# Attention scores with the mask added by a matmul and two heads in one product over 128 rows

## The chip, the core and the metric

The kernel runs on one core of a Trainium2 chip. The metric is the device time of one execution in microseconds (us). TensorE (PE) multiplies matrices and writes its results to PSUM; VectorE (DVE), ScalarE (ACT) and GpSimd (POOL) work elementwise; SyncE (SP) issues the DMAs. Each engine takes its instructions in the order of its own queue and waits on semaphores for the others.

## What is computed

Three stages follow each other: an attention over windows, a mixture of experts and a dense feed-forward layer. The change is in the first.

```python
# q, k, v: (4, 8, 576, 64), float32
scores = np.matmul(q, k.transpose(0, 1, 3, 2)) / np.sqrt(64)
rel = pos[:, None] - pos[None, :]
mask_plain = (rel >= 0) & (rel < 32)                     # heads 0 to 3
mask_dil = (rel >= 0) & (rel < 128) & (rel % 4 == 0)     # heads 4 to 7
scores = np.where(masks, scores, -1e9)
attn = np.exp(scores - scores.max(-1, keepdims=True))
attn = attn / (attn.sum(-1, keepdims=True) + 1e-9)
x = np.matmul(attn, v)          # then 2304 tokens x 512
# x: eight experts with gates normalised 8 times over rows and columns; then relu(x @ w_in)**2 @ w_out
```

## The kernel before

The host sorts positions by their remainder modulo 4 for the heads with the dilated mask, so that both masks become a band over neighbours. The 576 queries of a head are cut into 18 blocks of 32, and a block sees 64 keys (its own 32 and the 32 ahead). A *group* is one batch, four heads and six blocks; there are 4 x 2 x 3 = 24 groups.

`slot(i)` is the loop of the attention stage. It records, for different groups, the scores of group i (`att_scores`, L393), the exponential and the normalisation of group i - 1 (`att_exp`, `att_norm`), the product with v of group i - 3 (`att_pv`, L442), the transposes of group i - 2 (`att_tr`, L432), and matmuls that fill: either warm-ups on zeros (L999) or the first products of the experts (L587). Then SP gets the loads: q and k two groups ahead (`load_qk`), v (`load_v`), and parts of the expert weights or of the mask. The order in which the code is written is the order of each queue; no planner moves anything.

In `att_scores` each head of each block is a matmul of its own. Its rows are the 64 dimensions of the head, so heads 0 and 2 use rows 0 to 63 of the array and heads 1 and 3 rows 64 to 127, each with 32 columns. That is 24 products per group, and in float32 each is two matmuls with a weight load each; the trace counts 48. The weights are the 32 queries, the data that stream through are 64 keys, and the result is a PSUM tile `s` of 128 rows (4 heads x 32 queries) by 6 x 64, of which two banks rotate. On DVE, L413 scales the scores and adds the mask, a tile of 128 rows in SBUF with 0 or -1e30, and writes `ms`; L417 takes the maximum of each row. POOL subtracts it (L418) and ACT takes the exponential (L422). DVE sums (L427), adds 1e-9 (L428) and inverts (L429); POOL multiplies (L430). PE transposes (L437), ACT copies to `pts`, PE multiplies by v into `xt` (L452), and ACT copies the result into `xf` (L484), for the dilated heads at a step of 4 floats.

The mask comes in four pieces, the first ahead of the loop and three in slots 0 to 2. After the loop come the gates and then some 1800 us of expert and feed-forward products, nearly all of them PE's.

Of the kernel before, what the change touches and what calls it, by code (L numbers as in the profile page):

```python
# [10 lines left out]
F32 = mybir.dt.float32  # L11
F32R = mybir.dt.float32r
I32 = mybir.dt.int32
U32 = mybir.dt.uint32
AF = mybir.ActivationFunctionType
ALU = mybir.AluOpType
AX = mybir.AxisListType
PSUM = bass.MemoryType.PSUM

B, H, S, D = 4, 8, 576, 64  # L20
NTOK, DM = B * S, H * D
E, FE, FF = 8, 1024, 2048
QB = 32
PAD = 32
KB = QB + PAD
NB = S // QB
GB = 6
NM = NB // GB
QC = GB * QB
# [14 lines left out]
NEG = -1e30  # L44
# [4 lines left out]
def tile_kernel(ctx: ExitStack, tc: tile.TileContext, a):  # L49
    nc = tc.nc  # L50
    out = a["out"]
# [8 lines left out]
    xfp = att.enter_context(tc.tile_pool(name="xfp", bufs=1))  # L60
    qkv = att.enter_context(tc.tile_pool(name="qkv", bufs=2))
# [19 lines left out]
    every = slice(0, KC)  # L81

    ident = const.tile([128, 128], F32, name="ident")
    mask = xfp.tile([128, 4 * GB, KB], F32, name="mask")
    wg = xfp.tile([128, KC, 32], F32, name="wg")
    warm = xfp.tile([128, 128], F32, name="warm")

# [9 lines left out]
    bufs = {"s": 2, "xt": 2, "pt": 1, "mm": 3}  # L97
# [279 lines left out]
    q_t, k_t, v_t, e_t, pt_t, xt_t = {}, {}, {}, {}, {}, {}  # L377

    def load_qk(i):
        if i < NG:  # L380
            b, hg, m = groups[i]
            q_t[i] = qkv.tile([128, 2, QC], F32, tag="q", name="q", bufs=3)
            nc.sync.dma_start(q_t[i], a["q"][b, hg, m])
            k_t[i] = qkv.tile([128, 2, KCOLS], F32, tag="k", name="k", bufs=3)
            nc.sync.dma_start(k_t[i], a["k"][b, hg, m])

    def load_v(i):
        if i < NG:
            b, hg, m = groups[i]
            v_t[i] = qkv.tile([128, GB // 2, 4 * D], F32, tag="v", name="v", bufs=4)  # L390
            nc.sync.dma_start(v_t[i], a["v"][b, hg, m])

    def att_scores(i):  # L393
        _, hg, m = groups[i]
        qt, kt = q_t.pop(i), k_t.pop(i)
        ps = psum.tile([128, 512], F32, tag="s", name="s")[:, :GB * KB].rearrange("p (g k) -> p g k", g=GB)
        for g in range(GB):
            for head in range(4):
                pr, rows = head // 2, slice(D * (head % 2), D * (head % 2) + D)
                nc.tensor.matmul(  # L400
                    ps[QB * head:QB * head + QB, 2 * (g % 3) + g // 3, :],
                    qt[rows, pr, g * QB:g * QB + QB],
                    kt[rows, pr, g * QB:g * QB + KB],
                    start=True,
                    stop=True,
                )
        ms = at.tile([128, GB, KB], F32, tag="ms", name="ms", bufs=5)
        if hg == 0 and m > 0:
            mk = mask[:, 2:3, :].to_broadcast([128, GB, KB])
        else:  # L410
            k = m + 1 if hg else 0
            mk = mask[:, GB * k:GB * k + GB, :]
        nc.vector.scalar_tensor_tensor(  # L413
            out=ms, in0=ps, scalar=1.0 / float(np.sqrt(D)), in1=mk, op0=ALU.mult, op1=ALU.add,
        )
        mx = at.tile([128, GB, 1], F32, tag="mx", name="mx", bufs=3)
        nc.vector.tensor_reduce(out=mx[:, :, 0], in_=ms, axis=AX.X, op=ALU.max)  # L417
        nc.gpsimd.tensor_tensor(out=ms, in0=ms, in1=mx.to_broadcast([128, GB, KB]), op=ALU.subtract)  # L418
        e_t[i] = ms

    def att_exp(i):
        nc.scalar.activation(out=e_t[i], in_=e_t[i], func=AF.Exp)  # L422

    def att_norm(i):
        ex = e_t[i]
# [54 lines left out]
    def att_x(i):  # L480
        _, hg, _ = groups[i]
        for half, xt in enumerate(xt_t.pop(i)):
            for c, w, t0, step in att_parts(i, half):
                nc.scalar.copy(xf(slice(2 * hg, 2 * hg + 2), t0, w, step), xt[:, :, c:c + w])  # L484
# [444 lines left out]

    with tc.manual_schedule():  # L930
        nc.vector.memset(warm, 0.0)
        load_qk(0)
        nc.sync.dma_start(mask[:, :GB], a["mask"][:, :GB])
        load_qk(1)
        load_qk(2)
        nc.sync.dma_start(ident, a["ident"])

        ps = psum.tile([128, 512], F32, tag="s", name="s")
# [57 lines left out]
        def warm_up(n):  # L996
            ps = bank("mm") if n else None
            for _ in range(n):
                nc.tensor.matmul(ps, wr, xr, start=True, stop=True)  # L999
# [9 lines left out]
        def preparing(i):  # L1009
            for i0, z in ops:  # L1010
                if i >= i0:
                    next(z, None)
            for f in prep0.get(i, ()):
                f()

        def slot(i):
            if i < NG:
                att_scores(i)
            if 0 <= i - 4 < NG:
                att_x(i - 4)  # L1020
            if 0 <= i - 1 < NG:
                att_exp(i - 1)
                att_norm(i - 1)
            if 0 <= i - 3 < NG:
                att_pv(i - 3)
            between.get(i, lambda: None)()
            preparing(i)
            if 0 <= i - 2 < NG:
                att_tr(i - 2)
            for _ in range(filled.get(i, 0)):  # L1030
                next(filling)
            warm_up((4 if i < 6 else 2 if i < per + 4 else 3 if i < NG else 6) - filled.get(i, 0))
            if i:
                load_qk(i + 2)
            load_v(i)
            if parts:
                parts.pop(0)()
            if i < 3:
                cols = slice(GB * i + GB, GB * i + 2 * GB)
                nc.sync.dma_start(mask[:, cols], a["mask"][:, cols])  # L1040
            if i == 3:
                nc.sync.dma_start(wg, a["w_gate"])
            if i == 2:
                load_parts(0, 0)
            if i == 6:
                load_parts(0, 1)
            if i == 15:
                load_parts(1, 0)
# [194 lines left out]
def _layout(x):  # L1243
    q, k, v = x["q"], x["k"], x["v"]

    def order(z):
        lo = z[:, :4]
        hi = z[:, 4:].reshape(B, 4, S // DIL, DIL, D).transpose(0, 1, 3, 2, 4).reshape(B, 4, S, D)
        return np.stack([lo, hi], axis=1)

    qo, ko, vo = order(q), order(k), order(v)

    def pairs(z):
        return z.reshape(B, 2, 2, 2, S, D).transpose(0, 1, 3, 5, 2, 4)

    qs = pairs(qo).reshape(B, 2, 128, 2, NM, QC).transpose(0, 1, 4, 2, 3, 5)
    kz = pairs(ko).reshape(B, 2, 128, 2, S)
    kz = np.concatenate([np.zeros((B, 2, 128, 2, PAD), kz.dtype), kz], axis=-1)
    ks = np.stack([kz[..., m * QC:m * QC + KCOLS] for m in range(NM)], axis=2)

    vp = np.concatenate([np.zeros((B, 2, 4, PAD, D), v.dtype), vo], axis=3)
    vt = np.stack([vp[:, :, :, j * QB:j * QB + KB] for j in range(NB)], axis=3)
    vt = vt.reshape(B, 2, 4, NM, 2, GB // 2, KB, D).transpose(0, 1, 3, 4, 6, 5, 2, 7)
    vt = vt.reshape(B, 2, NM, 128, GB // 2, 4 * D)

    def first(w, n):
        return w.reshape(KC, 128, n, FC, 128).transpose(2, 1, 3, 0, 4).reshape(n, 128, KC * FB)

    def second(w, n):
        return w.reshape(n, FC, 128, DM).transpose(0, 2, 1, 3).reshape(n, 128, FC * DM)  # L1270

    w1 = np.concatenate([first(x["moe_w1"][e], SPE) for e in range(E)])
    w2 = np.concatenate([second(x["moe_w2"][e], SPE) for e in range(E)])
    kk = np.arange(KB)[None, :]
    qq = np.arange(QB)[:, None]
    band = (kk > qq) & (kk <= qq + PAD)

    def split_at(o):
        return band & ((qq < o) | (kk >= PAD + o))

    first_block, split, after_split = split_at(0), split_at(QB // 2), band & (kk >= QB // 2)
    masks = [
        z[3 * (k % 2) + k // 2]
        for z in (
            [first_block] + [band] * 5,
            [first_block, band, band, band, split, after_split],
            [band, band, band, first_block, band, band],
            [band, split, after_split, band, band, band],
        )
        for k in range(GB)  # L1290
    ]
    arrays = {
        "q": qs,
        "k": ks,
        "v": vt,
        "w_gate": np.pad(x["moe_w_gate"].reshape(KC, 128, E).transpose(1, 0, 2), ((0, 0), (0, 0), (0, 32 - E))),
        "w1": w1,
        "w2": w2,
        "w_in": first(x["moe2_w_in"], NS2),
        "w_out": second(x["moe2_w_out"], NS2),  # L1300
        "mask": np.tile(np.stack([np.where(m, 0.0, NEG).astype(np.float32) for m in masks], axis=1), (4, 1, 1)),
        "ident": np.eye(128, dtype=np.float32),
    }
    arrays = {n: np.ascontiguousarray(z) for n, z in arrays.items()}
    for n in ("w_in", "w_out"):
        arrays[n] = arrays[n].view(np.int64)
    return arrays
# [16 lines left out]
```

## Time and profile before

| | us |
|---|---|
| median of 3 runs (lowest, highest) | 1931.33 (1928.61, 1933.84) |
| the profiled execution | 1931.37 |
| its span | 1929.6 |
| PE busy in the span | 1902.9 (99%) |
| DVE busy | 1626.1 (84%) |
| ACT busy | 745.9 (39%) |
| POOL busy | 634.6 (33%) |

The profile was taken in one execution. A row that begins with a line number or an engine stands for instructions; `x` counts them. In a group of instructions the two numbers behind the bar are the busy time and the mean of one in nanoseconds, and what follows the next bar is the idle time of the engine just before them and what ended it. PEld is PE's weight load, which runs beside its matmuls. PEclk is the granted clock, 1.00 for 2.4 GHz. A matmul's end in the trace is modelled, so the distance between starts says more than a length.

### The profile page before, as it was taken

To read this page: it belongs to the slowest core of one execution; us is meant where nothing else is said; L and a number is where in the kernel's file an instruction comes from. 1 tells how busy PE (TensorE), PEld (TensorE's weight loads), DVE (VectorE), ACT (ScalarE), POOL (GpSimd) and SP (SyncE) were. 2 spreads that over 40 slices of the span, in tenths; PEclk is the share of its full clock that TensorE was granted. 3 is DMA by queue.
4 is the path that set the end of the run, shared out by engine and by line. 5 is a ranking of instruction groups with operands and counts; after the bars stand their busy time and mean duration, and the time that the engine had idled before them with its cause. 6 is when DMAs were issued, how large, how long until landed. Compare 5 with 4: busy or idle time off the path is not lost.

```text
span 1929.6 us, 29357 instructions
## 1 busy us (share of the span) xinstructions
PE 1902.9 (99%) x11008; PEld 1584.2 (82%) x11008; DVE 1626.1 (84%) x2336; ACT 745.9 (39%) x1242; POOL 634.6 (33%) x556
## 2 busy tenths in 40 slices
PE   8899999999999999999999999999999999999999
PEld 6677888888888888888788888888888878888887
DVE  5878889888888888888588998999999987776897
ACT  3553433333333333333334343333333355443443
POOL 4731433333333332223124233332323244331231
PEclk8999999999999999999999999999999999999999
DMA  8776666676666566666967677666667777779661
GB/s 265 220 293 229 248 243 242 255 283 256 251 256 230 217 236 251 233 236 242 395 233 302 250 256 264 255 253 242 223 249 267 300 290 259 249 284 400 226 244 66
DMA packets 166399, 491.84 MB, mean 255 GB/s; under 512 B 17248, under 2 KB 40176, under 8 KB 166256
## 3 DMA queue, kind: packets, MB, share of 16 engines
q1 hardware_dynamic: 166256, 489.96, 68.2%
q8 instruction: 87, 1.43, 0.3%
q14 instruction: 56, 0.46, 0.1%
HBM read 281.15 MB, written 208.74 MB: 254 GB/s over the span
## 4 chain that ended last, share of the span: by engine, by line
PE 93%; DVE 3%; DMA 1%; issue 1%; POOL 1%; ACT 0%; SPq 0%; DVEq 0%; ACTq 0%; POOLq 0%
PE mm L808 27%; PE pt L587 16%; PE s L587 11%; PE xt L587 11%; PE mm L891 11%; PE mm L768 5%; PE s L891 4%; PE xt L891 4%; PE xt L452 1%; PE s L400 1%; DVE acc L905 1%; DMA w_suml<-suml 1%; PE pt L437 0%; DMA w2l<-w_w2l 0%; PE mm L999 0%
## 5 line engine op out<-in xcount | busy, mean ns | idle before, releaser
L808 PE MATMUL mm<-w2h,g 128*128 128x512 f32 x1312 | 405.6, 390 | 0.2 <-DVE acc L834 0.2
L830 DVE SCALAR_TENSOR_TENSOR acc<-mm,ptile,acc 128x512 f32<-128x512 f32 x290 | 216.5, 747 | 103.6 <-PE mm L808 103.3
L808 PEld LDWEIGHTS mm<-w2h,g 128*128 128x128 f32 x1312 | 244.9, 188 | 50.2 <-DVE acc L834 0.3
L808 PE MATMUL mm<-w2l,g 128*128 128x512 f32 x656 | 255.4, 389 | 0.0
L698 POOL TENSOR_TENSOR r<-mix,r 128x512 f32<-128x512 f32 x39 | 51.1, 1311 | 543.5 <-DVE mix L687 428.7
L669 DVE TENSOR_TENSOR g<-r,g 128x512 fp32r<-128x512 f32 x156 | 158.9, 1020 | 47.3 <-ACT g L666 45.9
L186 POOL TENSOR_TENSOR sums<-raw 128x256 f32<-128x256 f32 x40 | 31.4, 785 | 475.1 <-DVE suml L172 414.6
L666 ACT CAST g<-r 128x512 fp32r<-128x512 f32 x156 | 96.7, 621 | 130.8 <-PE mm L891 109.7
L808 PEld LDWEIGHTS mm<-w2l,g 128*128 128x128 f32 x656 | 123.1, 188 | 25.8
L905 DVE TENSOR_TENSOR acc<-mm,acc 128x512 f32<-128x512 f32 x226 | 144.2, 678 | 0.0
L627 ACT ACTIVATE sg<-mm 128x512 fp32r<-128x512 f32 (+1 forms) x33 | 18.9, 574 | 273.7 <-PE mm L768 273.7
L587 PE MATMUL s<-x_hi,blkh 128*128 128x512 f32 x316 | 123.6, 391 | 1.1 <-ACT pt L721 1.1
L587 PE MATMUL xt<-x_hi,suml 128*128 128x512 f32 x316 | 123.0, 389 | 0.4 <-DMA suml<-w_suml 0.4
L587 PE MATMUL xt<-x_hi,sumh 128*128 128x512 f32 x316 | 123.3, 390 | 0.0
L587 PE MATMUL pt<-x_hi,sumh 128*128 128x512 f32 x316 | 123.2, 390 | 0.0
L587 PE MATMUL s<-x_lo,blkh 128*128 128x512 f32 x316 | 123.1, 390 | 0.0
L587 PE MATMUL s<-x_hi,blkl 128*128 128x512 f32 x316 | 123.0, 389 | 0.0
L587 PE MATMUL xt<-x_lo,sumh 128*128 128x512 f32 x316 | 123.0, 389 | 0.0
L587 PE MATMUL pt<-x_lo,sumh 128*128 128x512 f32 x316 | 123.0, 389 | 0.0
L587 PE MATMUL pt<-x_hi,suml 128*128 128x512 f32 x316 | 122.9, 389 | 0.0
L768 PE MATMUL mm<-xs,blkh 128*128 128x256 f32 x624 | 112.9, 280 | 1.2 <-DVE pT L557 1.2
L627 ACT ACTIVATE g<-s 128x512 fp32r<-128x512 f32 x95 | 59.0, 621 | 132.5 <-DVE s L738 66.7
(256 smaller groups left out, 4786.5 us busy)
## 6 DMA issues: line engine op xcount, KB each, us to landing
raw<-in_w SPq DMA_DIRECT2D x61, 512.0 KB, 6.9
blkh<-w_blkh SPq DMA_DIRECT2D x41, 512.0 KB, 3.7
blkl<-w_blkl SPq DMA_DIRECT2D x41, 512.0 KB, 4.5
sumh<-w_sumh SPq DMA_DIRECT2D x41, 512.0 KB, 4.4
suml<-w_suml SPq DMA_DIRECT2D x41, 512.0 KB, 5.7
w_blkh<-blkh SPq DMA_DIRECT2D x40, 512.0 KB, 6.5
w_blkl<-blkl SPq DMA_DIRECT2D x40, 512.0 KB, 6.9
w_sumh<-sumh SPq DMA_DIRECT2D x40, 512.0 KB, 6.3
```

The lines of the kernel that those rows point to most:

```text
L186: tt(out=c(sums, 0), in0=c(raw1, 2), in1=c(raw1, 3), op=ALU.add)
L400: nc.tensor.matmul(ps[QB * head:QB * head + QB, 2 * (g % 3) + g // 3, :], qt[rows, pr, g * QB:g * QB + QB], kt[rows, pr, g * QB:g * QB + K ...
L587: nc.tensor.matmul(ps, w[:, c], z[:, x, j], start=start and k == 0, stop=stop and k == 5, skip_group_check=True)
L627: after(k, lambda: nc.scalar.activation(out=ghi, in_=src, func=AF.Relu))
L666: after(k, lambda: nc.scalar.copy(b[:, 0], src))
L669: lambda: nc.vector.tensor_tensor(out=b[:, 1], in0=src, in1=b[:, 0].bitcast(F32), op=ALU.subtract),
L698: sub = lambda o, x, y: nc.gpsimd.tensor_tensor(out=o, in0=x, in1=y, op=ALU.subtract)
L768: nc.tensor.matmul(ps, w[:, c], z[:, kc], start=k == 0, stop=k == len(terms) - 1)
L808: nc.tensor.matmul(ps, g[:, c0 * 128:c0 * 128 + 128], wt[:, fc], start=k == 0, stop=k == 3 * FC - 1)
L830: nc.vector.scalar_tensor_tensor(out=dst, in0=ps, scalar=p, in1=dst, op0=ALU.mult, op1=ALU.add)
L891: nc.tensor.matmul(ps, w[wt][:, c], z[:, g], start=start and k == 0, stop=stop and k == 2, skip_group_check=True)
L905: nc.vector.tensor_tensor(out=o, in0=ps, in1=o, op=ALU.add)
```

## The change

The mask is no longer added on DVE. A tile `mask` of 32 rows holds, behind two slices with four unit matrices of 32 side by side (`spread_q`), the mask of each kind of block. One matmul with `spread_q` as weights writes the mask into all four heads' rows of the PSUM tile and opens the accumulation; it is in the type float32r, for which ACT casts the raw mask piece by piece (`round_mask`). The products of queries and keys then add to it.

These products take two heads at once. The weights are 64 columns, 32 queries of each of two heads, over all 128 rows: a head's queries stand in its own 64 rows and zeros in the others. For that q lies in three fixed tiles `q_zero`, whose zero halves DVE writes once at the start; each group's q comes in two DMAs of 64 rows. In such a tile the index of the pair and the block runs innermost, so that the 64 columns of a product's weights lie 12 floats apart. There are 12 products per group instead of 24, on array tiles of 128 rows by 64 columns.

DVE takes the maximum from PSUM and subtracts it there, which POOL did; the scale by 1/8 moves into the exponential. The mask comes in two DMAs ahead of the loop.

```diff
-    mask = xfp.tile([128, 4 * GB, KB], F32, name="mask")
+    mask = xfp.tile([QB, 4 * GB + 2, KB], F32R, name="mask")
+    mask_raw = xfp.tile([QB, 4 * GB + 2, KB], F32, name="mask_raw")
+    spread_q = mask[:, :2].rearrange("p g k -> p (g k)")
+    q_zero = [xfp.tile([128, 2, QB, 2, GB], F32, name=f"q{k}") for k in range(3)]
...
-            q_t[i] = qkv.tile([128, 2, QC], F32, tag="q", name="q", bufs=3)
-            nc.sync.dma_start(q_t[i], a["q"][b, hg, m])
+            q_t[i] = q_zero[i % 3]
+            for h in range(2):
+                rows = slice(D * h, D * h + D)
+                nc.sync.dma_start(q_t[i][rows, h], a["q"][b, hg, m][rows])
...
+    def round_mask(g0, g1):
+        nc.scalar.copy(mask[:, g0:g1], mask_raw[:, g0:g1])
+
     def att_scores(i):
...
+        k = m + 1 if hg else 0
+        if hg == 0 and m > 0:
+            mk = mask[:, 4:5, :].to_broadcast([QB, GB, KB])
+        else:
+            mk = mask[:, 2 + GB * k:2 + GB * k + GB, :]
+        nc.tensor.matmul(ps, spread_q, mk, start=True, stop=False, skip_group_check=True)
         for g in range(GB):
-            for head in range(4):
-                pr, rows = head // 2, slice(D * (head % 2), D * (head % 2) + D)
+            for pr in range(2):
                 nc.tensor.matmul(
-                    ps[QB * head:QB * head + QB, 2 * (g % 3) + g // 3, :],
-                    qt[rows, pr, g * QB:g * QB + QB],
-                    kt[rows, pr, g * QB:g * QB + KB],
-                    start=True,
+                    ps[2 * QB * pr:2 * QB * pr + 2 * QB, 2 * (g % 3) + g // 3, :],
+                    qt.rearrange("p h q r g -> p (h q) r g")[:, :, pr, g],
+                    kt[:, pr, g * QB:g * QB + KB],
+                    start=False,
                     stop=True,
+                    skip_group_check=True,
                 )
...
-        nc.vector.scalar_tensor_tensor(
-            out=ms, in0=ps, scalar=1.0 / float(np.sqrt(D)), in1=mk, op0=ALU.mult, op1=ALU.add,
-        )
...
-        nc.vector.tensor_reduce(out=mx[:, :, 0], in_=ms, axis=AX.X, op=ALU.max)
-        nc.gpsimd.tensor_tensor(out=ms, in0=ms, in1=mx.to_broadcast([128, GB, KB]), op=ALU.subtract)
+        nc.vector.tensor_reduce(out=mx[:, :, 0], in_=ps, axis=AX.X, op=ALU.max)
+        nc.vector.tensor_tensor(out=ms, in0=ps, in1=mx.to_broadcast([128, GB, KB]), op=ALU.subtract)
...
-        nc.scalar.activation(out=e_t[i], in_=e_t[i], func=AF.Exp)
+        nc.scalar.activation(out=e_t[i], in_=e_t[i], func=AF.Exp, scale=1.0 / float(np.sqrt(D)))
...
+        for z in q_zero:
+            nc.vector.memset(z[D:, 0], 0.0)
+            nc.vector.memset(z[:D, 1], 0.0)
+        nc.sync.dma_start(mask_raw[:, :GB + 2], a["mask"][:, :GB + 2])
+        round_mask(0, GB + 2)
         load_qk(0)
-        nc.sync.dma_start(mask[:, :GB], a["mask"][:, :GB])
         load_qk(1)
         load_qk(2)
+        nc.sync.dma_start(mask_raw[:, GB + 2:], a["mask"][:, GB + 2:])
...
-            if i < 3:
-                cols = slice(GB * i + GB, GB * i + 2 * GB)
-                nc.sync.dma_start(mask[:, cols], a["mask"][:, cols])
+            if 1 <= i < 4:
+                round_mask(GB * i + 2, GB * i + GB + 2)
```

On PE, around group 7 of the kernel before (`s` is the tile of the scores, `xt` of the product with v, `pt` of the transposes, `wr` and `xr` the warm-up's zeros):

```order
L999 MATMUL mm<-xr,wr 128x512 x2
L400 MATMUL s<-k,q 32x64 x24
L452 MATMUL xt<-pts,v 64x32 x24
L437 MATMUL pt<-ident,ms 128x128 x3
L999 MATMUL mm<-xr,wr 128x512 x2
```

And the same place in the changed kernel:

```order
L1010 MATMUL mm<-xr,wr 128x512 x2
L410 MATMUL s<-mask 128x384
L413 MATMUL s<-k,q_93 64x64 x12
L458 MATMUL xt<-pts,v 64x32 x24
L443 MATMUL pt<-ident,ms 128x128 x3
L1010 MATMUL mm<-xr,wr 128x512 x2
```

The mask's matmul stands ahead of the scores, whose products are half as many with twice the columns; the rest keeps its place.

On DVE, one group of the kernel before, from the masked copy of a group's scores to the next one's:

```order
L413 SCALAR_TENSOR_TENSOR ms<-s,mask 128x384
L417 TENSOR_REDUCE mx<-ms 128x6
L427 TENSOR_REDUCE rs<-ms 128x6
L428 TENSOR_SCALAR rs<-rs 128x6
L429 RECIPROCAL rs<-rs 128x6
```

And in the changed kernel:

```order
L423 TENSOR_REDUCE mx<-s 128x6
L424 TENSOR_TENSOR ms<-s,mx 128x384
L433 TENSOR_REDUCE rs<-ms 128x6
L434 TENSOR_SCALAR rs<-rs 128x6
L435 RECIPROCAL rs<-rs 128x6
```

Five instructions stay five: the masked copy is gone, and the subtraction of the maximum has come from POOL.

On SP, the start of the kernel before:

```order
L383 DMA q<-in_q 128x384
L385 DMA k<-in_k 128x448
L933 DMA mask<-in_mask 128x384
L383 DMA q<-in_q 128x384
L385 DMA k<-in_k 128x448
```

And of the changed kernel:

```order
L941 DMA mask_raw<-in_mask 32x512
L388 DMA q_92<-in_q 64x384 x2
L390 DMA k<-in_k 128x448
L388 DMA q_93<-in_q 64x384 x2
L390 DMA k<-in_k 128x448
```

The first k is the fourth DMA instead of the second, and every q is two.

## Rows read from the trace of the kernel before

**Rows 1.** The page, part 1: PE's busy time, share, count; its weight loads beside.

```profile
PE 1902.9 (99%) x11008; PEld 1584.2 (82%) x11008; DVE 1626.1 (84%) x2336; ACT 745.9 (39%) x1242; POOL 634.6 (33%) x556
```

**Rows 2.** Busy time by stretch: stretch, length, engines (count), PEclk, DMA share, GB/s.

```profile
50.00:100.00 50.00, 43.68 (x1363) 33.71 (x1361) 44.45 (x87) 30.00 (x81) 39.41 (x39) 1.00 0.66 206
```

**Rows 3.** Timeline of PE over one group: start, length, what.

```profile
50.16 0.87 PE L400 MATMUL s<-k,q 64*32 64x64 f32 x48
50.97 0.90 PE L452 MATMUL xt<-pts,v 64*64 64x32 f32 x48
51.80 0.55 PE L437 MATMUL pt<-ident,ms 128*128 128x128 f32 x3
52.10 0.93 PE L999 MATMUL mm<-xr,wr 128*128 128x512 f32 x3
52.97 0.88 PE L400 MATMUL s<-k,q 64*32 64x64 f32 x48
```

**Rows 4.** Waits of PE, 0 to 104 us: total, times, longest.

```profile
PE xt L452 <- issue: 4.1, 5, 1.1
PE pt L437 <- POOL ms L430: 4.1, 3, 1.8
PE s L400 <- issue: 2.8, 2, 2.4
PE xt L452 <- ACT xf L484: 1.2, 2, 0.8
```

**Rows 5.** The chain that ended last, in order of time: start, length, what.

```profile
5.26 1.44 PE s L400 x48
...
26.38 0.83 PE xt L452 x48
...
31.60 2.38 issue
...
38.96 1.43 PE xt L452 x48
...
205.85 1.36 PE mm L808 x6
```

**Rows 6.** Busy time by stretch again, around the stalls, columns as in rows 2.

```profile
23.86:31.60 7.74, 7.74 (x251) 6.09 (x251) 5.13 (x12) 3.95 (x13) 3.70 (x6) 1.00 0.80 239
...
80.43:84.17 3.74, 3.74 (x125) 2.97 (x125) 3.30 (x7) 2.36 (x7) 3.15 (x4) 1.00 0.53 165
...
34.40:44.50 10.10, 10.10 (x243) 8.32 (x246) 6.50 (x13) 3.41 (x10) 6.67 (x8) 0.50 0.64 200
45.00:50.00 5.00, 5.00 (x120) 3.45 (x118) 3.64 (x8) 3.41 (x10) 2.37 (x3) 1.00 0.68 222
```

**Rows 7.** DMA queues, 0 to 104 us: packets, MB, share.

```profile
q8 instruction: 20, 0.33, 1.3%
```

**Rows 8.** Timeline of PE at the second gate.

```profile
68.41 1.07 PE L490 MATMUL s<-xf,wg 128*32 128x512 f32 x8
69.40 0.81 PE L400 MATMUL s<-k,q 64*32 64x64 f32 x43
```

**Rows 9.** Groups of instructions with shapes apart, 0 to 400 us: DVE.

```profile
L413 DVE SCALAR_TENSOR_TENSOR ms<-s,mask 128x384 f32<-128x384 f32 x24 | 13.3, 554 | 20.4 <-PE s L400 19.3 <-DMA raw<-in_w 0.7
...
L536 DVE TENSOR_REDUCE scs<-ptile 128x8 f32<-128x144 f32 x8 | 3.4, 426 | 0.3
...
L528 DVE TENSOR_REDUCE srs<-ptile 128x18 f32<-128x144 f32 x8 | 2.4, 296 | 0.1
```

**Rows 10.** Timeline of ACT: copies for a plain and a dilated group.

```profile
20.72 0.55 ACT L484 COPY xf<-xt 128x192 f32<-128x192 f32 x2
...
30.93 0.86 ACT L484 COPY xf<-xt 128x192 f32<-128x192 f32 x2
```

**Rows 11.** Timeline of POOL and DVE in one group.

```profile
15.85 0.83 POOL L418 TENSOR_TENSOR ms<-ms,mx 128x384 f32<-128x384 f32 x1 [1.52 <-DVE mx L417]
16.27 0.44 DVE L428 TENSOR_SCALAR rs<-rs 128x6 f32<-128x6 f32 x1
```

**Rows 12.** Timeline of SP's issues at the start.

```profile
2.12 0.43 SPq L383 DMA_DIRECT2D q<-in_q  x1
```

## What I expect of the change

> **What bounds the kernel now.** I read the page first. TensorE (PE) is busy for 99% of the span [rows 1], so a change shows in the total only as far as it moves the time at which PE gets through the attention stage. The diff touches nothing behind that stage. So I asked next for the busy time by stretch: between 50 and 100 us PE is busy 43.68 of 50 us, VectorE (DVE) 44.45 and GpSimd (POOL) 39.41 [rows 2]. Three engines are nearly full there, and the order of events must say which one ends last.
>
> The timeline of one undisturbed group says it is PE [rows 3]. Scores start at 50.16, the products with v at 50.97, the transposes at 51.80, the filler at 52.10 and the next scores at 52.97. That is 2.81 us per group with no gap, made of 0.81 + 0.83 + 0.30 + 0.87. DVE needs less for its five instructions, and only where others are added does it end last.
>
> The waits of PE up to 104 us hold what comes on top: "issue" 4.1 + 2.8 = 6.9 us, the normalised weights from POOL 4.1 us, the copies of ScalarE (ACT) 1.2 us [rows 4]. "Issue" means that nothing the profile shows was awaited. The chain shows it in the middle of runs of equal matmuls, for example 2.38 us at 31.60 [rows 5]. Between two such stalls stand 125 + 126 matmuls and loads (80.43 to 84.17), or 251 + 251 (23.86 to 31.60) [rows 6]. [...] In that window the instruction queue moved 20 packets with 0.33 MB, about 16 KB each [rows 7]. I read these stalls as PE running out of instructions before the next block has come. A block is used up in 3.7 us at full pace, and with its stall of 0.81 us that is 4.5 us; the two blocks with 2.38 us come to 10.1 us, so a block can take about 5.1 us to arrive.
>
> The last extra cost follows the longest stall. PE did nothing from 31.60 to 33.98, and from 34.40 to 44.50 the granted clock is 0.50, the 1.2 GHz level, against 1.00 on both sides [rows 6]. The 48 matmuls with v then take 1.43 us instead of 0.83 [rows 5].
>
> **The change part by part.** The sum is made against the profiled execution, 1931.37 us (span 1929.6 and 1.8 around it). That run is as good as the median, 1931.33.
>
> *Mask product.* One more matmul per group, 384 columns from 32 rows. Six of 512 columns take 1.36 us, so 227 ns each [rows 5], and 384 columns take 0.17 us. It also adds a change of array shape. The existing change from the filler to the scores costs 0.87 - 3 x 0.227 = 0.19 us [rows 3]. A second one is bounded by 0.08 (half of it) and 0.25; I take 0.18, its nearest row. Together 0.35 us per group, on PE's path.
>
> *Scores.* Now 48 matmuls (two per product) on four array tiles take 0.81 us, 12 per tile, 68 ns each [rows 3]. After the change there are 24 on two tiles of 128 rows by 64 columns, again 12 per tile. Two column halves that share all rows can run side by side: the gate's eight matmuls of 128 rows by 32 columns and 512 columns of data take 68.41 to 69.40, 0.99 us, where one after the other at 227 ns or more they would take 1.8 us [rows 8]. So the products alone would again need 12 x 68 = 0.82 us. The weight load may need more. It brings 64 columns, as in the products with v, where 12 loads per tile take 0.83 us, 69 ns each. But its elements now lie 12 floats, 48 bytes, apart. No row of before shows a weight load of that kind. Two rows show what such steps do to other engines. The same 144 elements of one tile are reduced in 296 ns when read in a row (L528) and in 426 ns at a step of 32 bytes (L536), 0.90 ns more per element [rows 9]. Two copies of ACT into the same tile take 0.55 us together when they write in a row and 0.86 us at a step of 16 bytes [rows 10]. So the load is bounded by 69 ns and 69 + 64 x 0.90 = 127 ns, the scores by 0.83 and 1.52 us. I take 1.52, because both rows with such steps, one of reading and one of writing, show nearly a doubling, and I found no row of an engine's access to SBUF with such a step and without the cost. That is +0.71 us per group.
>
> [...]
>
> PE's path so grows by 24 x (0.35 + 0.71) = 25.4 us, and by 0.3 us for the first group, which runs at the lower clock.
>
> *Instruction stalls.* A group held 2 x (48 + 48 + 3 + 2 to 4) = about 204 matmuls and loads; it now holds 46 fewer, about 158. [...] The 6.9 us go, and with the long stall the stretch at 1.2 GHz. PE's work in it took 10.1 us, and at the ratio of the 48 matmuls (0.83 / 1.43) it takes 5.9. So -6.9 and -4.2. If a stall of that length still falls somewhere, 4.2 us stay; this is inside the range.
>
> [...]
>
> *DVE, POOL, ACT.* On DVE the masked copy out of PSUM (554 ns, L413) becomes a subtraction out of PSUM of the same size, and the maximum reads PSUM instead of SBUF [rows 9]. I cost both at nothing; each engine's cover is the longer group on PE. The bank of the scores is now free only after the second of the two; the next scores but one use it, a group later, which hides the 0.55 us. POOL loses its subtraction, 0.83 us per group. This frees DVE too: the small L428 ends as POOL's subtraction ends (16.27 + 0.44 = 16.71 against 15.85 + 0.83 = 16.68), so 0.44 us become about 0.2 [rows 11]. ACT gets four casts of the mask, three of 384 columns at about 0.5 us in groups 1 to 3, ahead of the exponential on its queue; ACT has room there. PE's waits for POOL and ACT, 4.1 + 1.2 = 5.3 us, come from a chain of DVE and POOL that is now shorter while PE arrives about 1 us later per group. I leave 0.3: -5.0.
>
> *Issues and start.* SP issues one more DMA per group at 0.43 us [rows 12]; behind it wait k, v and the weights. They are loaded two groups ahead, over 5 us, which hides 0.43. If that cover is gone the whole of it falls on a group. At the start two more issues stand ahead of the first k, 0.9 us, behind warm-up matmuls that run without a gap into the scores at 5.26 [rows 5]. I take +0.4 between 0 and 0.9. The mask's bytes shrink, which I count as nothing.
>
> Sum: +25.4 +0.3 -6.9 -4.2 -5.0 +0.4 = +10.0 us, so 1941.4 us.
>
> **The rivals.**
> *The step costs nothing.* The loads then take 69 ns and the scores +0.02 us. PE grows by 24 x 0.37 = 8.9, +0.3. A block lasts 5.2 us, so the stalls still go (-6.9, -4.2); of PE's waits 1.7 stay (-3.6); +0.4. That is -5.1, 1926.3 us. For it: every weight load of before runs at a rate that grows with its columns and hides behind products. Against it: rows 9 and 10. It decides the sign: from a load of about 92 ns on the kernel is slower.
>
> *The two halves' loads don't overlap.* Then 24 loads of 127 ns follow each other, 3.05 us instead of 1.52, +37 us: 1978 us. The change would not do what it says, two heads at once. Against it: the products with v, whose 48 loads of 64 columns in 0.83 us need four at a time.
>
> *The stalls stay.* If they are not a matter of instructions, +11.1 us on either case: 1952 or 1937 us. For it: other transfers were busy then. [...]
>
> **How the numbers follow.** The forecast gets 0.52, the free step 0.36, the loads one after the other 0.04, the stalls that stay 0.08. A measurement of this kernel can tell about 0.3%, 5.8 us, from no change, so the lines are 1925.6 and 1937.1. The forecast's own range, with loads of 100 to 135 ns, the second shape change at 0.08 to 0.25 and the low clock still there or not, is 1934 to 1948; 0.44 of its 0.52 lies above the upper line. The free step ranges from 1922 to 1931, and 0.17 lies below the lower line. With 0.04 and half of 0.08 above, slower gets 0.52, faster 0.17, same 0.31. A range of 1924 to 1948 leaves out about 0.07 below and 0.1 above.
>
> **What would show it.** The row of the scores' loads: 24 per group over about 1.5 us says forecast, over 0.8 the free step. A group's period in the timeline: 3.9 us or 3.2. PE's waits: "issue" near zero, at a granted clock of 1.00 after 7 us. The small L434, which takes L428's place, at about 0.2 us. The forecast is wrong if the scores keep their 0.81 us, or if stalls of 1 to 2 us still cut runs of equal matmuls.

## The result and the profile after

The changed kernel takes 1942.38 us (median of 4 runs, 1941.74 to 1943.23), the kernel before beside it 1932.02. The ratio is 1.0056, with a 95% interval of 1.0044 to 1.0068: slower by about half a per cent, one microsecond from the forecast. That agreement is partly luck, as the steps below show: the scores became dearer than forecast, and more waiting went away than forecast.

The page of the changed kernel, span and part 1 (it answers to [rows 1]):

```profile
span 1941.4 us, 28258 instructions
...
PE 1928.0 (99%) x10456; PEld 1607.8 (83%) x10456; DVE 1619.9 (83%) x2342; ACT 748.5 (39%) x1246; POOL 615.4 (32%) x532
```

PE executes 552 matmuls fewer and is busy 25 us longer. Where they went shows in the timeline of one group (start, length, what), to be laid beside [rows 3]:

```profile
56.07 0.43 PE L410 MATMUL s<-mask 32*128 32x384 f32 x1
56.44 1.84 PE L413 MATMUL s<-k,q 128*64 128x64 f32 x24
58.21 0.90 PE L458 MATMUL xt<-pts,v 64*64 64x32 f32 x48
59.04 0.55 PE L443 MATMUL pt<-ident,ms 128*128 128x128 f32 x3
59.35 0.94 PE L1010 MATMUL mm<-xr,wr 128*128 128x512 f32 x3
60.22 0.44 PE L410 MATMUL s<-mask 32*128 32x384 f32 x1
```

Read from start to start, the mask's product holds PE for 0.37 us and the scores for 1.77, where 48 matmuls took 0.81 (the trace counts matmuls, two to a product). All else in the group is as before, and its period is 4.15 us instead of 2.81.

PE's waits from 0 to 118 us, the view that answers to [rows 4], hold one row, the wait for the first operand of the program:

```profile
PE s L951 <- DVE warm L937: 1.1, 1, 1.1
```

The stops marked "issue" and the waits for POOL and ACT are all gone. DVE and POOL are no longer near the limit (columns as in [rows 2]):

```profile
50.00:100.00 50.00, 50.00 (x907) 40.13 (x907) 32.32 (x74) 25.79 (x70) 20.64 (x19) 1.00 0.66 200
```

A mark behind the attention stage is the start of eight gate matmuls with 512 columns. The first fence is before, the second the changed kernel, the third a second profile of the changed kernel, told of below.

```profile
104.74 1.06 PE L490 MATMUL s<-xf,wg 128*32 128x512 f32 x8
```

```profile
118.43 1.06 PE L496 MATMUL s<-xf,wg 128*32 128x512 f32 x8
```

```profile
115.91 1.07 PE L496 MATMUL s<-xf,wg 128*32 128x512 f32 x8
```

The stage ends 13.7 us later, or 11.2. From the mark to the end of the span it is 1824.9, 1823.0 and 1824.1 us, and 1823.4 to 1825.8 in the experiments with intervals: what follows varies by some 2 us from profile to profile, in no order that the change explains. So the difference is made in the attention stage, as forecast.

### The profile page after: what moved, and what is told of

It is laid out like the page before. It is cut to its first block, busy times and chain, and to the rows that moved or that the text cites. A ratio compares the mean times of both kernels' runs of the same rounds, so it can differ in the third digit from the quotient of the medians.

```text
span 1941.4 us, 28258 instructions
## 1 busy us (share of the span) xinstructions
PE 1928.0 (99%) x10456; PEld 1607.8 (83%) x10456; DVE 1619.9 (83%) x2342; ACT 748.5 (39%) x1246; POOL 615.4 (32%) x532
## 4 chain that ended last, share of the span: by engine, by line
PE 95%; DVE 3%; DMA 1%; ACT 1%; issue 0%; POOL 0%; SPq 0%; DVEq 0%; ACTq 0%; POOLq 0%
PE mm L814 28%; PE pt L593 16%; PE s L593 11%; PE xt L593 11%; PE mm L897 10%; PE mm L774 6%; PE s L897 4%; PE xt L897 4%; PE s L413 2%; PE xt L458 1%; PE mm L1010 1%; PE pt L443 1%; DVE acc L911 1%; PE s L410 0%; DMA w2l<-w_w2l 0%; PE mm L593 0%
```

## Experiments

**The theory and its rival.** The theory: the weight loads are slow because their 64 elements lie 48 bytes apart, and the two column halves still load side by side. The rival: two halves that share all 128 rows load one after the other, whatever the step. The two read the same 1.77 us differently, as 12 x 147 ns or as 24 x 73.5.

**The step alone.** The queries come from memory with the zeros in them, so that the order of the 64 weights can be chosen freely. Y is the step in floats: 12 (the control), 4, 2 and 1.

```
-    q_zero = [xfp.tile([128, 2, QB, 2, GB], F32, name=f"q{k}") for k in range(3)]
+    q_zero = [xfp.tile([128, 12 // Y, 2 * QB, Y], F32, name=f"q{k}") for k in range(3)]
...
-            for h in range(2):
-                rows = slice(D * h, D * h + D)
-                nc.sync.dma_start(q_t[i][rows, h], a["q"][b, hg, m][rows])
+            nc.sync.dma_start(q_t[i], a["q"][b, hg, m])
...
-                    qt.rearrange("p h q r g -> p (h q) r g")[:, :, pr, g],
+                    qt[:, (GB * pr + g) // Y, :, (GB * pr + g) % Y],
...
-        for z in q_zero:
-            nc.vector.memset(z[D:, 0], 0.0)
-            nc.vector.memset(z[:D, 1], 0.0)
```

The expectations count the trace's matmuls and call them products: 24 of them are a group's scores.

> The control for the run with 4 bytes: the same queries with zeros from memory in one transfer, but the weights 48 bytes apart as in the changed kernel. Theory and rival both expect the scores at 1.77 us and a total of 1942 within 3. Another time would mean that the way the zeros come, not the step, matters.

> As the control, with the weights 16 bytes apart. If every element that lies in another stretch of 16 bytes costs the same, the scores take 1.77 us as at 48 bytes and the total is 1942; if the cost grows with the distance, about 1.1 us and 1926. The rival (halves one after the other): 1.77 us at any distance, the 4 bytes included.

> As the control, with the weights 8 bytes apart. If the cost goes by stretches of 16 bytes that are touched (32 instead of 16 or 64), the scores take about 1.1 to 1.3 us, the total 1926 to 1931. If any step at all costs the whole of it: 1.77 us and 1942. If 8 bytes are free: 0.8 us, 1921.

> The queries come from memory with the zeros for the other head already in them, one transfer per group, and the 64 weights of a score product lie in a row (4 bytes apart instead of 48). Nothing else differs from the changed kernel; no fixed buffers are filled with zeros. Theory (the step makes the weight loads slow): the 24 score products of a group take 0.8 to 0.9 us instead of 1.77, a group's period falls from 3.92 to about 3.0, the clock rises early again, and the total is 1942.4 - 24 x 0.9 = 1921, at most 1927. Rival (two column halves that share all 128 rows load one after the other, whatever the step): the scores keep 1.77 us and the total stays at 1942 within 3.

The timelines of PE at the mask's product, the scores and the products with v: 48 bytes, then 16, 8 and 4.

```profile
49.41 0.44 PE L408 MATMUL s<-mask 32*128 32x384 f32 x1
49.78 1.83 PE L411 MATMUL s<-k,q 128*64 128x64 f32 x24
51.54 0.90 PE L456 MATMUL xt<-pts,v 64*64 64x32 f32 x48
```

```profile
56.27 1.65 PE L411 MATMUL s<-k,q 128*64 128x64 f32 x24
57.86 0.90 PE L456 MATMUL xt<-pts,v 64*64 64x32 f32 x48
```

```profile
48.31 0.94 PE L411 MATMUL s<-k,q 128*64 128x64 f32 x24
49.18 0.90 PE L456 MATMUL xt<-pts,v 64*64 64x32 f32 x48
```

```profile
44.59 0.92 PE L411 MATMUL s<-k,q 128*64 128x64 f32 x24
45.44 0.90 PE L456 MATMUL xt<-pts,v 64*64 64x32 f32 x48
```

| step | scores, start to start | total, us (ratio to the kernel before) |
|---|---|---|
| 48 bytes | 1.76 us | 1943.21, ratio 1.0058 [1.0041, 1.0075] |
| 16 bytes | 1.59 us | 1938.41 (one run) |
| 8 bytes | 0.87 us | 1929.92 (one run) |
| 4 bytes | 0.85 us | 1927.36, ratio 0.9977 [0.9966, 0.9988] |

The step is the cause, and nearly all of the cost comes between 8 and 16 bytes; 1.59 us at 16 bytes is neither of the two times expected. The control's scores and total are those of the changed kernel (1.76 and 1.77 us), so where the zeros come from costs nothing that can be told. The total at 8 bytes says less than its scores: behind the mark that profile takes 1827.1 us, 3.4 of them at PEclk 0.50 from 1545.75 us on.

These times don't say whether a step of 8 bytes costs nothing or whether its cost is hidden. Counted in stretches of 16 bytes, a unit that no run singles out, a load touches 16, 32, 64 and 64 of them at the four steps. In the traces the matmuls of one column half start 58, 60, 120 and 133 to 137 ns apart. That 120 is twice 60, as 64 is twice 32, fits a price for each stretch that is touched, about 1.9 ns by this estimate; at 4 bytes such a load would be hidden behind another limit, for the products with v, whose 64 weights lie in a row, start 58 to 59 ns apart on a tile too. Then 8 bytes are free only up to that limit. No run here tells this reading from a cliff, and neither of the two gives the 48 bytes.

With the weights in a row the kernel is faster than before, but the total falls by 15.9 us only, where 24 x 0.91 = 21.8 were to be had. The waits of the run with 4 bytes show some of the 6 us that are missing:

```profile
...
PE s L411 <- issue: 1.3, 1, 1.3
PE s L946 <- DVE warm L935: 1.1, 1, 1.1
PE pt L441 <- POOL ms L434: 0.9, 2, 0.8
PE pt L441 <- issue: 0.2, 1, 0.2
```

As the group gets shorter, stops marked "issue" and waits for POOL come back, 2.4 us together, and behind the longest stop a stretch of 3.4 us at PEclk 0.50 (first row below), which by the starts in the trace costs some 1.5 us:

```profile
37.79:41.20 3.41, 3.41 (x30) 2.32 (x28) 2.19 (x5) 1.85 (x5) 2.13 (x2) 0.50 0.99 342
41.20:45.00 3.80, 3.80 (x79) 2.31 (x79) 2.62 (x6) 2.74 (x6) 1.77 (x3) 1.00 0.74 252
```

**One half of the array.** The same kernels with 48 and 4 bytes, but with only one pair of heads multiplied.

```
-            for pr in range(2):
+            for pr in range(1):
```

> The control with 48 bytes, but only one of the two pairs of heads is multiplied: 12 score products per group on one column half instead of 24 on two. The other pair's scores are left out. If the two halves load side by side (147 ns for a load), 12 take as long as 24 did: 1.76 us, and the total stays near 1943. If their loads go one after the other (73 ns each), 12 take 0.88 us and the total falls by about 20 us, to 1923 or to what then bounds instead.

> The same with the weights in a row: 12 score products per group on one column half, the other pair of heads left out. Side by side (71 ns for a load and product): 12 take 0.85 us as 24 did, total near 1927. One after the other (35 ns): 0.43 us. Where this one keeps its time and the one with 48 bytes halves, the wide step is what puts the loads of the two halves in a row.

```profile
48.85 1.83 PE L411 MATMUL s<-k,q 128*64 128x64 f32 x12
50.61 0.90 PE L456 MATMUL xt<-pts,v 64*64 64x32 f32 x48
```

```profile
45.15 0.91 PE L411 MATMUL s<-k,q 128*64 128x64 f32 x12
45.99 0.90 PE L456 MATMUL xt<-pts,v 64*64 64x32 f32 x48
```

Twelve matmuls take 1.76 us at 48 bytes (the first fence) and 0.84 at 4 bytes, as long as twenty-four do; the totals, 1942.58 and 1925.36 (one run each), stay too. The rival falls: the halves load side by side at either step, and a load with its matmul takes 147 ns at 48 bytes and 70 at 4, the two ends of the run shared out. One way out would be left to it: that on one half alone each load waits for the matmul ahead of it. The matmul would then have to last as long as the load, 73 ns at one step and 35 at the other, though the same keys stream through.

**Each part of the change alone.** First the mask by a product, with the queries and the 48 score matmuls of before:

```
-            for pr in range(2):
+            for head in range(4):
+                pr, rows = head // 2, slice(D * (head % 2), D * (head % 2) + D)
                 nc.tensor.matmul(
-                    ps[2 * QB * pr:2 * QB * pr + 2 * QB, 2 * (g % 3) + g // 3, :],
-                    qt.rearrange("p h q r g -> p (h q) r g")[:, :, pr, g],
-                    kt[:, pr, g * QB:g * QB + KB],
+                    ps[QB * head:QB * head + QB, 2 * (g % 3) + g // 3, :],
+                    qt[rows, pr, g * QB:g * QB + QB],
+                    kt[rows, pr, g * QB:g * QB + KB],
```

> The mask by a product alone: the scores keep the 48 products of 64 rows of the kernel before, and its queries. PE's instructions per group do not fall (one more product and load). Theory: +0.37 us per group for the mask's product, 24 x 0.37 = 8.9; the instruction stalls (6.9 us) and the stretch at 1.2 GHz behind the longest of them stay; PE's waits for POOL and ACT (5.3) mostly go: 1932 + 8.9 - 4 = 1937. If the stalls came not from the number of instructions but from the chain of DVE and POOL or from transfers, they go here too and the total is about 1926.

It took 1930.81 us, ratio 0.9996 [0.9986, 1.0005]: no difference that can be told, and 6 us less than expected. PE's waits, 0 to 115 us:

```profile
PE s L411 <- issue: 2.9, 3, 1.7
PE xt L456 <- issue: 2.8, 4, 1.4
...
PE pt L441 <- POOL ms L434: 1.1, 2, 0.8
...
PE xt L456 <- ACT xf L488: 0.2, 1, 0.2
```

The stops marked "issue" stay, 5.7 us in seven, while the waits for POOL and ACT fall from 5.3 to 1.3 us. This run and the one with 4 bytes do the same on every engine but PE, which has 96 matmuls and loads for a group's scores here and 48 there; the latter has 1.5 us of such stops in two, although it moves more bytes. The run with 4 bytes on one half has 24 fewer again, in groups as long (3.2 us), with the same transfers: it has one stop, of 0.6 us. Between the last stops lie equal numbers of matmuls and loads again (stretches of this run, columns as in [rows 2]):

```profile
82.69:86.48 3.79, 3.79 (x126) 2.91 (x126) 2.51 (x6) 2.19 (x6) 1.97 (x2) 1.00 0.56 177
86.86:90.80 3.94, 3.94 (x125) 3.02 (x125) 2.90 (x7) 1.97 (x5) 2.43 (x3) 1.00 0.62 199
91.00:95.64 4.64, 4.64 (x126) 2.96 (x125) 3.20 (x7) 2.96 (x7) 3.75 (x5) 1.00 0.76 264
```

So the stops follow PE's count of instructions and the pace at which it uses them up: 250 to 252 matmuls and loads lie between two stops here, used up in 3.8 to 4.6 us, and 251 in 3.7 us in the kernel before [rows 6]. The packets of the instruction queue, some 16 KB each, go by the same count: 20 for 2 x 2530 matmuls and loads up to the mark of the kernel before [rows 7], 16 for 2 x 1978 in the changed kernel, about 250 to a packet. In the changed kernel a group with three fillers has 2 x 79 matmuls and loads in 4.15 us, so that 251 of them last 6.6 us, and no stop is left. That a stop is the wait for the next packet is the author's reading; no run shows it by itself.

Then the pairing alone, from the fixed buffers at 48 bytes, with mask and subtraction as before; and the same with the weights in a row, the queries as in the run with 4 bytes.

```
-        nc.tensor.matmul(ps, spread_q, mk, start=True, stop=False, skip_group_check=True)
...
-                    start=False,
+                    start=True,
...
+        nc.vector.scalar_tensor_tensor(
+            out=ms, in0=ps, scalar=1.0 / float(np.sqrt(D)), in1=mk, op0=ALU.mult, op1=ALU.add,
+        )
-        nc.vector.tensor_reduce(out=mx[:, :, 0], in_=ps, axis=AX.X, op=ALU.max)
-        nc.vector.tensor_tensor(out=ms, in0=ps, in1=mx.to_broadcast([128, GB, KB]), op=ALU.subtract)
+        nc.vector.tensor_reduce(out=mx[:, :, 0], in_=ms, axis=AX.X, op=ALU.max)
+        nc.gpsimd.tensor_tensor(out=ms, in0=ms, in1=mx.to_broadcast([128, GB, KB]), op=ALU.subtract)
```

> The pairing alone: 24 score products over 128 rows from the fixed buffers, 48 bytes apart, while the mask is added by DVE and the maximum subtracted by POOL as in the kernel before. Theory: scores 1.77 us (+0.95 x 24 = 22.8 us, +1.4 at the start), the instruction stalls and the low clock go (-11.1), PE's waits for POOL and ACT shrink because PE is later: 1932 + 13 - 4 = 1941, and 1934 if all of the mask's 8.9 us comes off the changed kernel. Instruction stalls that stay would speak against the number of instructions as their cause.

> The pairing alone with the weights in a row and the queries with zeros from memory; mask and subtraction as in the kernel before. Theory (the step is what is slow): scores 0.8 to 0.9 us with half the instructions, no stalls for instructions, no low clock behind them: 1932 - 6.9 - 4.2 = 1921 if PE's waits for POOL and ACT do not grow; these 5 us may double, since a group is now short on PE: 1921 to 1927. Rival (halves one after the other): 1.77 us, 1936 to 1941.

At 48 bytes: 1935.35 us, ratio 1.0014 [1.0005, 1.0023], with 1.77 us for the scores and, in PE's waits, no stop marked "issue". In a row: 1925.14 us, ratio 0.9963 [0.9950, 0.9975], the fastest of all and faster than both kernels. It keeps PE free of the mask's 8.9 us, and pays with waits (0 to 98 us):

```profile
PE pt L437 <- POOL ms L430: 3.9, 3, 1.5
PE xt L452 <- issue: 1.5, 2, 0.9
PE xt L452 <- ACT xf L484: 1.4, 3, 0.8
PE s L940 <- DVE warm L931: 1.1, 1, 1.1
PE s L400 <- issue: 0.9, 1, 0.9
PE s L400 <- DMA k<-in_k: 0.4, 1, 0.4
```

Each part alone moves the end of the stage by less than it adds to PE's work or takes from it, since PE meets other limits there. With the mask's product alone PE has 8.9 us more to do, but 4.0 us of waits and 1.2 us of stops go, and the stage ends 3.2 us later (the mark is at 107.93 instead of 104.74); why the medians of the totals don't show these 3.2 us stays open. Without the mask's product POOL's and ACT's waits stay: 3.9 and 1.4 us above, 4.1 and 1.2 in the kernel before.

**The clock at the start.** In the first profile of the changed kernel PE's four fillers, 512 columns each, took 2.0 us in the first two groups, as at the lower level (PEclk 0.50), and 1.1 from the third on. The traces give the two levels as 0.50 and 1.00; the frequencies by which the texts on record name them stand in none. The granted clock is on record from 13.96 us on, at 1.00:

```profile
5.80 1.89 PE L413 MATMUL s<-k,q 128*64 128x64 f32 x24
7.62 2.07 PE L1010 MATMUL mm<-xr,wr 128*128 128x512 f32 x4
...
12.05 2.06 PE L1010 MATMUL mm<-xr,wr 128*128 128x512 f32 x4
...
16.49 1.17 PE L1010 MATMUL mm<-xr,wr 128*128 128x512 f32 x4
```

> The changed kernel once more, unchanged. In its first profile the granted clock rose to 1.00 only at 13.96 us, in the control with 48 bytes at 6.4 us. If the fixed buffers or the order of the first loads cause it, it is late again and the end of the attention stage stays 2 us behind the control; if it is chance, the clock rises at 6 to 7 us here. No difference of the total is expected: 1942 to 1943.

The second profile (1941.82 us) has the fillers at the higher level from the first group, and the clock on record at 1.00 from 4.68 us on:

```profile
5.35 1.83 PE L413 MATMUL s<-k,q 128*64 128x64 f32 x24
7.12 1.20 PE L1010 MATMUL mm<-xr,wr 128*128 128x512 f32 x4
```

The late rise belongs to the one execution, not to the kernel, and costs the 2.5 us between the two marks shown above.

## Why the prediction held, and where its steps failed

Against the mark, in us, with the second profile as the one without the late clock:

| step | predicted | measured |
|---|---|---|
| mask's product | 24 x 0.35 = +8.4 | 24 x 0.37 = +8.9 |
| scores | 24 x 0.71 = +17.0 | 24 x (1.77 - 0.81) = +23.0 |
| first group, start, stops, low clock, waits | +0.3 +0.4 -6.9 -4.2 -5.0 = -15.4 | -20.7, what is left |
| sum | +10.0 | +11.2 at the mark (first profile +13.7); spans +10.4 (+11.8) |

**The mask's product** was right, its second change of array shape included (0.18, from the nearest row).

**The scores** had the right mechanism and the wrong size. That the step decides, that the halves load side by side, and that the sign hangs on the load's price are shown by the runs. The term that failed is the price of a wide step: 0.90 ns per element, taken from a reduction on DVE [rows 9], gave 127 ns per load; it was 147, that is 147 - 70 = 77 ns more for 64 elements, 1.2 ns each. The row taken from DVE had a step of 32 bytes, between the 16 bytes (1.59 us, 132 ns a load) and the 48 measured here. The bound set at 127 was so too low, and the scores fell outside it.

**What goes away** was priced too low as well, by 5.3 us, and this made up for most of the 6.0 us above. All three items went, as forecast: the stops, the stretch at PEclk 0.50 and the waits. But each stop costs more than the idle time that the view of the waits gives it. In the kernel before:

```profile
17.45 0.53 PE L452 MATMUL xt<-pts,v 64*64 64x32 f32 x18
19.11 0.66 PE L452 MATMUL xt<-pts,v 64*64 64x32 f32 x30 [1.12 <-issue]
19.70 0.55 PE L437 MATMUL pt<-ident,ms 128*128 128x128 f32 x3
```

From 17.45 to 19.70 are 2.25 us for 48 matmuls that else take 0.83: the stop cost 1.42 us, and 1.12 is shown as a wait. Over the seven such stops the difference is 0.2 to 0.4 us each, 2.1 together. The first group was to lose 0.3 us; it gained 0.6, since before it ran at the lower level (1.44 us for its scores [rows 5], 0.81 later on) and the scores of the changed kernel hardly depend on that level (1.89 us at it, 1.84 above it). The 0.4 us for the start are not seen, PE goes from the warm-ups into the mask's product without a gap, and of the 0.3 us of waits that were to stay nothing did. That is 3.7 of the 5.3 us. The starts in the two traces hold the rest: the five waits for POOL and ACT cost 6.3 us in the kernel before and not the 5.3 shown, the stretch at PEclk 0.50 about 4.4 and not 4.2, and the warm-ups and first fillers of the second profile, in which the clock rose earlier, take 0.4 us less. The last is luck of an execution. The runs put the cause of the stops where the prediction had it: counted by the 251 of [rows 6], the forecast's 3.87 us a group gave 6.1 us from one stop's place to the next, against the 5.1 us estimated from the longest stop; the measured group gives 6.6, and no stop is left.

**DVE, POOL and the issues** were free, as costed. The small step on DVE went from 0.44 us [rows 11] to 0.17 (L434, timeline of DVE), as forecast:

```profile
64.12 0.17 DVE L434 TENSOR_SCALAR rs<-rs 128x6 f32<-128x6 f32 x1
```

**The rivals.** The free step, 1926.3 us, is what the kernel with 4 bytes does (1927.36): its condition was not met, its total was right and its scores nearly so (0.04 us more per group instead of 0.02), though not all of the stops and the low clock went, as it had them go: 1.5 us of stops and 3.4 us at PEclk 0.50 stayed. The 5.2 us that it gives a block of instructions rest on a size that no run shows; by the 251 from stop to stop they are 5.1 us, no more than the 5.1 us estimated from the longest stop. What spoke for it is in the trace of before: loads of 32, 64 and 128 columns read 114, 144 and 188 ns (L400, L452, L808), beside the matmuls. The loads one after the other are excluded by the runs on one half. Stops that stay are excluded by the waits.

## What to carry to other kernels

Lay the stationary operand out so that the elements of one load lie in a row, or at most 8 bytes apart: at 16 bytes the load takes nearly twice as long (1.59 us for the scores against 0.87), and a layout chosen for the transfer's sake takes back what the merged products give. Merging small matmuls also halves the instructions, and this can be worth more than array time where PE runs short of them: with the weights in a row the 24 matmuls of the scores take no less time than the 48 before (0.85 and 0.81 us), and the pairing alone still made the kernel 6.8 us faster (1925.14 against 1931.98). A stop inside a run of matmuls is to be priced from start to start, not by the idle time that is shown (1.42 us against 1.12 above).

## What the runs showed of the hardware

The weight loads with a wide step hardly depend on PE's clock. With weights 48 bytes apart the 24 matmuls read 1.89 us beside fillers at the lower level and 1.84 at the higher (rows above). With weights in a row they follow the clock: 1.55 us in the stretch at 0.50, 0.92 at 1.00 (the run with 4 bytes, the second row as shown above).

```profile
39.74 1.55 PE L411 MATMUL s<-k,q 128*64 128x64 f32 x24
```

So it is not PE's clock that limits a wide load; what does, no run here shows. A step of 8 bytes adds 0.02 us to the scores and one of 16 bytes 0.74 (0.87 and 1.59 us against 0.85 in a row). At 48 bytes they take 0.17 us more than at 16 (1.76 us), and no run here says why.
